# One level of Strassen's method for the two layers with 768 outputs, in a kernel of attention and two feed-forward layers

## The chip, the cores and the metric

The kernel runs on one core of a Trainium2 chip. The time is that of the device for one execution, in microseconds (us); of several runs the median is given.

## What is computed

```python
def reference(**kwargs):
    attn_out = _attn_ref(**attn_kwargs)          # causal attention, B=2, H=12, S=448, D=64
    x = np.ascontiguousarray(attn_out.transpose(0, 2, 1, 3)).reshape(B * S, H * D)
    x = _moe_ref(x=x, **moe_kwargs)
    return _moe2_ref(x=x, **moe2_kwargs)

def _moe_ref(x, w_in, w_out):                    # x 896 x 768, w_in 768 x 2048, w_out 2048 x 768
    h = x @ w_in
    g = h * np.clip(h + 3.0, 0.0, 6.0) / 6.0
    return (g @ w_out).astype(np.float32)

def _moe2_ref(x, w_gate, w_val, w_out, rms_g):   # w_gate, w_val 768 x 1536, w_out 1536 x 768
    rms = np.sqrt(np.mean(x * x, axis=-1, keepdims=True) + 1e-06)
    xn = x / rms * rms_g
    g = xn @ w_gate
    return (g * (1.0 / (1.0 + np.exp(-g))) * (xn @ w_val) @ w_out).astype(np.float32)
```

The weights arrive in float64, the rest in float32.

## The kernel before

The 896 tokens are two groups g of 448: the first and the second halves of both sequences. Activations lie transposed, tiles of 128 features x 448 tokens. A product in float32 accuracy is three matmuls on rounded halves (`mm3`, lines 179 to 188: hi x hi, hi x lo, lo x hi), each with a 128 x 128 weight tile and 448 columns.

The stages, in the order of `products` (line 472):

- attention, in 24 units of a pair of heads, one sequence and one group; the first matmuls of `ff1_in` are mixed in from the thirteenth unit on
- `ff1_in`: h = x w_in for group 0, then 1; 16 output tiles of 6 input tiles each; `ff1_relu`, `ff1_mul` form g, `ff1_high` and `ff1_low` split it into `ghi` and `glo`
- `ff1_out`: y = g w_out, group by group; 6 output tiles of 16 input tiles; `ff1_y` and `ff1_ylow` scale y by rms_g, split it, and POOL adds up its squares; `rms_sum`, `rms_root`, `rms_inv` form the inverse root
- `ff2_in`: gate and value (tile f), 12 x 2 x 2 output tiles of 6 input tiles; `ff2_gate`, `ff2_silu`, `ff2_val`, `ff2_high`
- `ff2_out`: 6 output tiles x 2 groups of 12 input tiles; `ff2_store`.

Weights come in pieces of 768 columns (six 128 x 128 tiles). `w_load` (line 107) loads float64; `w_split` turns it into float32 on ACT (Prelu for the high word, a byte operation for the low bits; for w_in that one is on POOL), `w_join` on DVE; `w_halves` (ACT) and `w_low` (DVE) make `whi` and `wlo`. The layers that go through their weights twice store the float32 pieces to DRAM (`w_keep`) and load them back for group 1.

The order is written out by hand. The program is built in steps; `at(delay, fn, ...)` records fn at a later step, and each step issues AFTER = 9 matmuls (BESIDE = 4.8 beside attention). A piece n is split one step after the first use of piece n - 3 (`w_tile`, line 169), halved a step later (two, where it has to be joined), its `wlo` made a step after that, and `w_low` asks for the next load. Every engine works its instructions off in this order, SP its DMA issues too; four buffers hold `whi` and `wlo`, three the raw pieces.

Of the kernel before, what the change touches and what calls it, by code (L numbers as in the profile page):

```python
# [9 lines left out]
F32 = mybir.dt.float32  # L10
# [11 lines left out]
NK = DM // 128  # L22
# [6 lines left out]
NSLOT = 82  # L29
# [3 lines left out]
BESIDE, AFTER = 4.8, 9  # L33
APART = 4
# [11 lines left out]
def fused_kernel(ctx: ExitStack, tc, qa, qb, ka, kb, v, w_in, w_out, w_gate, w_val, w_out2, rms_g, out):  # L46
# [53 lines left out]
    srcs, kept = [], {}  # L100
# [4 lines left out]
    srcs += [w_out2[n] for n in range(NF2)]  # L105
# [3 lines left out]
    state = {"load": 0, "split": 0}  # L109

    def w_load():
        n = state["load"]
        if n >= len(srcs):
            return
        state["load"] += 1
        if srcs[n] is None:
            c = wpool.tile([128, 768], F32, tag="c", name=f"c{n}", bufs=NC_BUF)
            nc.sync.dma_start(c, kept.pop(n))
            plain[n] = c
            return  # L120
        t = wpool.tile([128, 768, 2], U32, tag="raw", name=f"raw{n}", bufs=NRAW)
        nc.sync.dma_start(t.rearrange("p n t -> p (n t)"), srcs[n].bitcast(U32))
        raws[n] = t

    def w_split():
# [37 lines left out]
    def w_low(n, c):  # L163
        hi, lo = splits[n]
        nc.vector.tensor_sub(lo, c, f32(hi))  # L165
        if n >= NRAW:
            w_load()
# [11 lines left out]
    def mm3(ps, w, x, first, last):  # L179
# [3 lines left out]
        nc.tensor.matmul(ps, whi, xhi, start=first, stop=False)  # L183
        yield
        nc.tensor.matmul(ps, whi, xlo, start=False, stop=False)  # L185
        yield
        nc.tensor.matmul(ps, wlo, xhi, start=False, stop=last)  # L187
        yield


# [167 lines left out]
    def ff1_high(g, m, t):  # L358
        hi = slot([128, NT], f"ghi{g}_{m}", F32R)
        lo = slot([128, NT], f"glo{g}_{m}", F32R)  # L360
        nc.scalar.copy(hi, t)
        gs[g, m] = (hi, lo)
        at(1, ff1_low, hi, lo, t, nc.vector if g == 0 else nc.gpsimd)

    def ff1_low(hi, lo, t, engine=None):
        (engine or nc.gpsimd).tensor_sub(lo, t, f32(hi))  # L366

    def ff1_out(g, w0):

# [16 lines left out]

# [209 lines left out]
```

## Time and profile before

| | |
|---|---|
| median of 3 runs (lowest, highest) | 600.92 us (600.91, 601.79) |
| the profiled execution's own time | 601.82 us |
| its span, first to last instruction | 600.0 us |
| PE busy | 591.4 us, 99% |
| PE weight loads, DVE, ACT, POOL busy | 86%, 51%, 57%, 23% |
| mean granted TensorE clock | 0.997 of full speed |
| bytes moved by DMA | 92.98 MB, 155 GB/s over the span |

The profile is of one execution. Busy time of PE counts matmuls that overlap, so a row's mean duration is not the time between two of them. "Idle before" is the time an engine stood still just before the instructions of a row, with the engine, tile and line that ended most of it. The chain is followed back from the last instruction, at each step to what released it.

### The profile page before, as it was taken

The numbers are of one execution on the slowest core, as the hardware profiler recorded it, in microseconds if no ns is written. First come the engines' busy times: TensorE is split into PE (matmuls) and PEld (weight loads), VectorE is DVE, ScalarE is ACT, GpSimd is POOL, SyncE is SP. The second block draws the span as 40 slices with busy tenths as digits, with TensorE's granted clock in tenths as the row PEclk, the third lists the DMA queues.
The fourth block names the chain that finished last, engine by engine and source line by source line (L and its number), as shares of the span: only waits on it lengthen the run. The fifth ranks groups of instructions, "written<-read, shape, count | busy, mean of one in ns | idle before, by whom it ended". The sixth has DMA issues, their size and how long they took to land.

```text
span 600.0 us, 8836 instructions
## 1 busy us (share of the span) xinstructions
PE 591.4 (99%) x3192; PEld 518.8 (86%) x3192; DVE 307.2 (51%) x579; ACT 341.2 (57%) x652; POOL 137.7 (23%) x172
## 2 busy tenths in 40 slices
PE   8899999999999999999999999999999999999997
PEld 6557777778899999999999999999999999999996
DVE  4666767676444456563435565555544455333310
ACT  6998888787455688764335764445555544333300
POOL 4665454542033320010001011111111111000000
PEclk9999999999999999999999999999999999999999
DMA  8958776652233489863353433333333333344000
GB/s 222 277 192 253 226 247 217 215 182 85 74 108 116 182 306 330 319 226 124 101 185 140 154 128 117 112 117 107 106 106 105 106 105 106 121 139 148 32 32 31
DMA packets 32075, 92.98 MB, mean 155 GB/s; under 512 B 4640, under 2 KB 13792, under 8 KB 32032
## 3 DMA queue, kind: packets, MB, share of 16 engines
q1 hardware_dynamic: 31600, 92.08, 46.1%
q8 instruction: 25, 0.41, 0.3%
q10 hardware_dynamic: 432, 0.34, 0.2%
q14 instruction: 18, 0.15, 0.1%
HBM read 77.07 MB, written 15.34 MB: 154 GB/s over the span
## 4 chain that ended last, share of the span: by engine, by line
PE 94%; ACT 4%; POOL 1%; DVE 1%; issue 1%; POOLq 0%
PE f L183 10%; PE f L187 10%; PE f L185 10%; PE h L187 7%; PE y L183 7%; PE h L183 7%; PE h L185 7%; PE y L187 6%; PE y L185 6%; PE o L183 5%; PE o L187 5%; PE o L185 5%; PE s L241 3%; PE o L318 3%; PE t L292 3%; ACT sm L258 3%
## 5 line engine op out<-in xcount | busy, mean ns | idle before, releaser
L159 ACT CAST whi<-c 128x768 fp32r<-128x768 f32 x100 | 83.5, 835 | 89.5 <-DVE c L147 57.7
L165 DVE TENSOR_TENSOR wlo<-c,whi 128x768 fp32r<-128x768 f32 x100 | 99.7, 998 | 38.4 <-ACT whi L159 36.1
L183 PE MATMUL f<-yhi,whi 128*128 128x448 f32 x288 | 105.8, 367 | 0.0
L187 PE MATMUL f<-yhi,wlo 128*128 128x448 f32 x288 | 104.9, 364 | 0.0
L185 PE MATMUL f<-ylo,whi 128*128 128x448 f32 x288 | 104.0, 361 | 0.0
L147 DVE SCALAR_TENSOR_TENSOR c<-c,raw 128x768 uint32<-128x768 uint32 x68 | 66.9, 984 | 22.0 <-ACT raw L142 15.5
L187 PE MATMUL h<-xh,wlo 128*128 128x448 f32 x192 | 72.0, 375 | 0.0
L276 POOL TENSOR_SCALAR sm<-sm,st 112x112 f32<-112x112 f32 (+1 forms) x96 | 55.7, 598 | 69.1 <-ACT pt L302 28.3
L185 PE MATMUL h<-xl,whi 128*128 128x448 f32 x192 | 70.9, 369 | 0.0
L183 PE MATMUL y<-ghi,whi 128*128 128x448 f32 x192 | 70.5, 367 | 0.0
L183 PE MATMUL h<-xh,whi 128*128 128x448 f32 x192 | 70.4, 367 | 0.0
L187 PE MATMUL y<-ghi,wlo 128*128 128x448 f32 x192 | 70.0, 365 | 0.0
L185 PE MATMUL y<-glo,whi 128*128 128x448 f32 x192 | 69.3, 361 | 0.0
L366 POOL TENSOR_TENSOR slo<-u,shi 128x448 fp32r<-128x448 f32 x24 | 28.6, 1193 | 147.6 <-ACT shi L444 138.5
L138 ACT ACTIVATE c<-raw 128x768 f32<-128x768 f32 x68 | 61.4, 903 | 0.0
L187 PEld LDWEIGHTS f<-yhi,wlo 128*128 128x128 f32 x288 | 53.9, 187 | 5.4 <-issue 0.2
L185 PEld LDWEIGHTS f<-ylo,whi 128*128 128x128 f32 x288 | 54.1, 188 | 4.0
L183 PEld LDWEIGHTS f<-yhi,whi 128*128 128x128 f32 x288 | 54.1, 188 | 3.7 <-issue 0.2
L183 PE MATMUL o<-shi,whi 128*128 128x448 f32 x144 | 52.9, 367 | 0.0
L187 PE MATMUL o<-shi,wlo 128*128 128x448 f32 x144 | 52.3, 363 | 0.0
L258 ACT ACTIVATE sm<-sm,st 112x112 f32<-112x112 f32 (+3 forms) x96 | 49.7, 528 | 4.2 <-DVE st L251 4.2
L185 PE MATMUL o<-slo,whi 128*128 128x448 f32 x144 | 52.0, 361 | 0.0
(62 smaller groups left out, 866.9 us busy)
## 6 DMA issues: line engine op xcount, KB each, us to landing
raw<-in_w_out SPq DMA_DIRECT2D x28, 768.0 KB, 4.8
raw<-in_w_in SPq DMA_DIRECT2D x16, 768.0 KB, 5.5
kept<-c SPq DMA_DIRECT2D x32, 384.0 KB, 2.8
c<-kept SPq DMA_DIRECT2D x32, 384.0 KB, 3.1
raw<-in_w_gate SPq DMA_DIRECT2D x12, 768.0 KB, 4.3
raw<-in_w_val SPq DMA_DIRECT2D x12, 768.0 KB, 4.2
k<-in_kb SPq DMA_DIRECT2D x24, 112.0 KB, 4.6
v<-in_v SPq DMA_DIRECT2D x12, 224.0 KB, 3.6
```

Source lines behind the costliest of these rows:

```text
L138: nc.scalar.activation(c, f32(high), AF.Prelu, scale=2.0 ** -112, alpha=2.0 ** 32)
L147: nc.vector.scalar_tensor_tensor(bits, bits, 3, z, ALU.logical_shift_left, ALU.bitwise_or)
L159: nc.scalar.copy(hi, c)
L165: nc.vector.tensor_sub(lo, c, f32(hi))
L183: nc.tensor.matmul(ps, whi, xhi, start=first, stop=False)
L185: nc.tensor.matmul(ps, whi, xlo, start=False, stop=False)
L187: nc.tensor.matmul(ps, wlo, xhi, start=False, stop=last)
L241: nc.tensor.matmul(ps[:C, o:o + n], tq[64 * j:64 * j + 64, i * C:(i + 1) * C], tk[64 * j:64 * j + 64, 0:n], start=True, stop=True)
L258: nc.scalar.activation(dst, dst, AF.Exp, scale=-1.0, bias=st[u][:, 0, c:c + 1], accum_out=st[u][:, 1, c:c + 1])
L276: nc.gpsimd.tensor_scalar(t[:, o:o + n], t[:, o:o + n], c, 1.0, op0=ALU.mult, op1=ALU.mult)
L292: nc.tensor.transpose(banks[-1][:C, o:o + C], t[:, o0 + kc * C:o0 + (kc + 1) * C], ident[:C, :C])
L366: (engine or nc.gpsimd).tensor_sub(lo, t, f32(hi))
```

## The change

Both layers with 768 outputs are computed by one level of Strassen's method (in Winograd's form). The matrix of activations is cut by token group and by the parity of its input tiles, the weights by the parity of input tile and output tile. For a pair p of input tiles, A11 and A12 are the even and the odd tile of group 0, A21 and A22 those of group 1. The sums s1 = A21 + A22, s3 = A11 - A21, s2 = s1 - A11, s4 = A12 - s2 are formed on POOL (`sums_first`, `sums_second`, `sums_third`). Seven products replace eight: q = 1: A11 B11; 2: A12 B21; 5: s1 (B12 - B11); 6: s2 times B22 less the block of 5; 7: s3 times the block of 6 less B11; 3: s4 B22; 4: A22 times B21 less the block of 6. They stand outermost (ORDER1, ORDER2), each over 3 pairs n of output tiles and all input tiles of a parity; `combine` adds them up on DVE, or lets them accumulate in the same PSUM bank.

The float64 weights are turned to float32 once, cut by parity and kept in DRAM (`b_prepare`, `b_narrow`, `b_join`, `b_keep`): w_out beside attention and `ff1_in`, w_out2 beside `ff2_in`. A piece of a product is then one load, or two loads and a subtraction on POOL (tile pair); the blocks of products 5 and 6 are stored for later use. Pieces of `ff1_out` have 512 columns. The split of the activations moves from right behind their making to a product ahead (`a_split`, `a_low`; tiles `ahi`, `alo`).

```diff
-NSLOT = 82
+WIDE1, HALVES1 = 512, 2
+WIDE2 = 768
+ORDER1 = (1, 2, 5, 6, 7, 3, 4)
+ORDER2 = (1, 5, 6, 7, 3, 4, 2)
+BLOCKS = {1: (1,), 2: (2,), 3: (22,), 5: (12, 1), 6: (22, 5), 7: (6, 1), 4: (2, 6)}
+PREP1, APART1 = 108, 3.5
+NSLOT = 78
...
-    for a in (w_in, w_out):
-        srcs += [a[n] for n in range(NP1)] + NP1 * [None]
+    srcs += [w_in[n] for n in range(NP1)] + [("in", n) for n in range(NP1)]
+    srcs += [(1, p, n, h) for p in ORDER1 for n in range(NN) for h in range(HALVES1)]
...
+        return wpool.tile([128, 768, 2], U32, tag="raw", name=name, bufs=NRAW + 1)
...
+            for p in BLOCKS[q]:
+                found.append(kept[stage, p, k][:, h * wide:(h + 1) * wide])
...
+            t = f32(raw_tile(f"pair{n}").rearrange("p n t -> p (n t)"))
+            both = [t[:, :wide], t[:, 768:768 + wide]]
+        for t, src in zip(both, found):
+            nc.sync.dma_start(t, src)
+        plain[n] = both
...
-            at(1, w_halves, n, plain.pop(n))
+            c, *other = plain.pop(n)
+            if other:
+                nc.gpsimd.tensor_sub(c, c, other[0])
+                stage, q, k, h = srcs[n]
+                if q in (5, 6):
+                    at(1, b_keep, stage, q, k, h * c.shape[1], c)
+            at(1, w_halves, n, c)
...
+    def b_narrow(stage, column, first, raw, wide, beside):
+        narrowed(f32(raw[:, :wide, 1]), raw, beside)
+        at(1, b_join, stage, column, first, raw, wide)
...
+    def b_keep(stage, p, n, o, t):
...
+        nc.sync.dma_start(kept[stage, p, n][:, o:o + wide], t)
...
-        at(1, ff1_high, g, m, t)
+        left1[g, m] = t
+        if g == 1 and m % 2 == 1:
+            at(1, sums_first, left1, m // 2)
...
+    def a_split(left, q, p):
...
+        nc.scalar.copy(hi, src)
+        halves[which, q, p] = (hi, lo)
+        at(1, a_low, left, q, p, key, hi, lo, src)
+
+    def a_low(left, q, p, key, hi, lo, src):
+        nc.vector.tensor_sub(lo, src, f32(hi))
...
+    def strassen(which, order, kps, w0, pieces, after):
...
+        for i, q in enumerate(order):
+            if i + 1 < len(order):
+                for p in range(kps):
+                    at(LEAD[which] + p, a_split, left, order[i + 1], p)
+            for n in range(NN):
...
+                for p in range(kps):
+                    w = w_tile(w0 + (i * NN + n) * pieces + p // per, p % per)
+                    yield from mm3(ps, w, halves[which, q, p], first and p == 0, p == kps - 1, not first)
...
+                at(1, combine, which, q, n, ps, after)
...
+        elif q == 4:
+            t = held.pop(("f", n))
+            nc.vector.tensor_add(t, ps, t)
+            at(1, after, 1, 2 * n, t)
...
-                    for k in range(NK):
-                        yield from mm3(ps, w_tile(w0 + 2 * m + n, k), ys[g, k], k == 0, k == NK - 1)
+                    ks = (1, 3, 5, 0, 2, 4)
+                    for k in ks:
+                        yield from mm3(ps, w_tile(w0 + 2 * m + n, k), ys[g, k], k == ks[0], k == ks[-1])
...
-        yield from ff1_out(0, 2 * NP1)
-        yield from ff1_out(1, 3 * NP1)
-        yield from ff2_in(4 * NP1)
-        yield from ff2_out(4 * NP1 + 2 * NF2)
+        yield from strassen(1, ORDER1, NF1 // 2, OUT1, HALVES1, ff1_y)
+        for i in range(2 * NK):
+            at(6 + 6 * i, b_prepare, 2, w_out2, i // 2, i % 2, False)
+        yield from ff2_in(IN2)
+        yield from strassen(2, ORDER2, NF2 // 2, OUT2, 1, ff2_store)
...
+        for i in range(3 * NK):
+            column = (0, 2, 4, 1, 3, 5)[i // 3]
+            plan[int(PREP1 + APART1 * i)].append((0, b_prepare, 1, w_out, column, i % 3, column % 2 == 0))
```

How the instructions stand. First POOL in `ff1_out`, before: behind the low halves of g it only has the sums of squares (tile sq).

```order
L366 TENSOR_TENSOR glo1_14_2719<-t1_14_2686,ghi1_14_2718 128x448
L366 TENSOR_TENSOR glo1_15_2756<-t1_15_2724,ghi1_15_2755 128x448
L394 TENSOR_TENSOR sq0_0_2811<-sq0_0_2811,sq0_1_2895 128x448
L394 TENSOR_TENSOR sq0_0_2811<-sq0_0_2811,sq0_2_2990 128x448
L394 TENSOR_TENSOR sq0_0_2811<-sq0_0_2811,sq0_3_3074 128x448
```

And POOL there now, from the last sum of activations (line 498) on through the pieces 44 to 50, of the products 5 and 6:

```order
L498 TENSOR_TENSOR t0_15_2198<-t0_15_2198,t0_14_2141 128x448
L165 TENSOR_TENSOR pair44_3032<-pair44_3032 128x512
L165 TENSOR_TENSOR pair45_3056<-pair45_3056 128x512
L603 TENSOR_TENSOR sq0_0_3040<-sq0_0_3040,sq0_2_3108 128x448
L165 TENSOR_TENSOR pair46_3080<-pair46_3080 128x512
L165 TENSOR_TENSOR pair47_3127<-pair47_3127 128x512
L603 TENSOR_TENSOR sq0_0_3040<-sq0_0_3040,sq0_4_3180 128x448
L165 TENSOR_TENSOR pair48_3152<-pair48_3152 128x512
L165 TENSOR_TENSOR pair49_3175<-pair49_3175 128x512
L165 TENSOR_TENSOR pair50_3219<-pair50_3219 128x512
```

POOL now has a subtraction of two weight blocks for each piece of the products 5, 6, 7 and 4, and some sums of squares stand between them.

Second DVE at the handover from `ff1_out` to `ff2_in`, before (c66 and c67 are the second and third piece of `ff2_in`, ylo1_5 the last low half of y):

```order
L165 TENSOR_TENSOR wlo65_3650<-c65_3624,whi65_3649 128x768
L147 SCALAR_TENSOR_TENSOR c66_3652<-c66_3652,raw66_3590 128x768
L165 TENSOR_TENSOR wlo66_3679<-c66_3652,whi66_3678 128x768
L389 SCALAR_TENSOR_TENSOR ylo1_5_3700<-y1_5_3586,gvec_74,yhi1_5_3681 128x448
L147 SCALAR_TENSOR_TENSOR c67_3685<-c67_3685,raw67_3637 128x768
L428 TENSOR_TENSOR t0_0_3717<-f0_0_0_3669,sq0_0_2811 128x448
```

DVE there now; piece 74 is the first of `ff2_in`, v1_1 the bank of product 4 for the second pair of output tiles, e1_1 its result:

```order
L215 TENSOR_TENSOR wlo73_3909<-pair73_3848,whi73_3908 128x512
L190 SCALAR_TENSOR_TENSOR c74_3928<-c74_3928,raw74_3885 128x768
L576 TENSOR_TENSOR e1_1_2926<-v1_1_3878,e1_1_2926 128x448
L617 RECIPROCAL sq0_0_3040<-sq0_0_3040 128x448
L190 SCALAR_TENSOR_TENSOR c75_3944<-c75_3944,raw75_3902 128x768
L215 TENSOR_TENSOR wlo74_3958<-c74_3928,whi74_3957 128x768
L597 SCALAR_TENSOR_TENSOR ylo1_2_3980<-e1_1_2926,gvec_74,yhi1_2_3960 128x448
```

And ACT there now:

```order
L588 ACTIVATE yhi1_0_3904<-e1_0_2859,gvec_74 128x448
L590 ACTIVATE sq1_0_3906<-e1_0_2859 128x448
L209 CAST whi73_3908<-pair73_3848 128x512
L181 ACTIVATE c74_3928<-raw74_3885 128x768
L185 ACTIVATE raw74_3885<-raw74_3885 128x768
L613 ACT_TABLE_LOAD
L613 ACTIVATE sq0_0_3040<-n0_3920,eps_73 128x448
L181 ACTIVATE c75_3944<-raw75_3902 128x768
L185 ACTIVATE raw75_3902<-raw75_3902 128x768
L209 CAST whi74_3957<-c74_3928 128x768
```

The reciprocal of group 0, whose square root stands on ACT in front of `whi74`, has moved to between the join and the low half of `ff2_in`'s first piece; before, that of group 0 stood far ahead of this handover.

## Rows read from the trace of the kernel before

**Rows 1.** The page: busy time of the engines, and the chain that ended last.

```profile
PE 591.4 (99%) x3192; PEld 518.8 (86%) x3192; DVE 307.2 (51%) x579; ACT 341.2 (57%) x652; POOL 137.7 (23%) x172
...
PE 94%; ACT 4%; POOL 1%; DVE 1%; issue 1%; POOLq 0%
```

**Rows 2.** By stage: length, busy PE, PEld, DVE, ACT, POOL; clock, DMA share, GB/s.

```profile
47.00:155.00 108.00, 108.00 (x710) 83.31 (x708) 74.36 (x175) 86.10 (x203) 47.20 (x57) 1.00 0.61 196
155.00:216.00 61.00, 61.00 (x302) 56.56 (x303) 28.33 (x39) 34.72 (x55) 19.12 (x14) 1.00 0.43 143
216.00:333.00 117.00, 117.00 (x579) 108.15 (x578) 60.10 (x63) 66.80 (x92) 13.27 (x11) 1.00 0.61 213
333.00:509.00 176.00, 176.00 (x871) 162.84 (x870) 90.31 (x121) 91.87 (x127) 28.65 (x24) 1.00 0.33 112
509.00:597.00 88.00, 87.52 (x433) 80.80 (x431) 24.93 (x32) 20.93 (x28) 1.15 (x1) 1.00 0.24 83
```

**Rows 3.** Matmuls of tiles y and f (first, last start); rms in the chain.

```profile
L183 PE MATMUL y<-ghi,whi x192: 367/367/368, 216.3 to 332.9; 128*128 128x448 f32 x192
...
L183 PE MATMUL f<-yhi,whi x288: 367/367/368, 333.5 to 508.4; 128*128 128x448 f32 x144
...
281.77 0.75 PE n L400 x2
```

**Rows 4.** Groups by line and shape: busy, mean ns | idle before, releasers.

```profile
L165 DVE TENSOR_TENSOR wlo<-c,whi 128x768 fp32r<-128x768 f32 x100 | 99.7, 998 | 38.4 <-ACT whi L159 36.1
L159 ACT CAST whi<-c 128x768 fp32r<-128x768 f32 x100 | 83.5, 835 | 89.5 <-DVE c L147 57.7 <-PE y L185 19.3 <-PE o L185 11.2
...
L147 DVE SCALAR_TENSOR_TENSOR c<-c,raw 128x768 uint32<-128x768 uint32 x68 | 66.9, 984 | 22.0 <-ACT raw L142 15.5 <-POOL raw L140 3.5 <-ACT c L138 2.7
L138 ACT ACTIVATE c<-raw 128x768 f32<-128x768 f32 x68 | 61.4, 903 | 0.0
...
L142 ACT ACTIVATE raw<-raw 128x768 uint32<-128x768 uint8 x52 | 46.1, 887 | 0.0
...
L366 POOL TENSOR_TENSOR slo<-u,shi 128x448 fp32r<-128x448 f32 x24 | 28.6, 1193 | 147.6 <-ACT shi L444 138.5 <-DMA raw<-in_w_val 9.1
...
L366 DVE TENSOR_TENSOR glo<-t,ghi 128x448 fp32r<-128x448 f32 x16 | 9.9, 618 | 1.9 <-ACT ghi L361 1.7
...
L382 ACT ACTIVATE yhi<-y,gvec 128x448 fp32r<-128x448 f32 x12 | 7.5, 628 | 17.2 <-PE y L187 17.2
...
L384 ACT ACTIVATE sq<-y 128x448 f32<-128x448 f32 x12 | 6.4, 531 | 0.0
L408 DVE RECIPROCAL sq<-sq 128x448 f32<-128x448 f32 x2 | 5.9, 2953 | 6.2 <-ACT sq L404 6.2
...
L404 ACT ACT_TABLE_LOAD x2 | 2.6, 1283 | 0.0
...
L404 ACT ACTIVATE sq<-n,eps 128x448 f32<-128x448 f32 x2 | 1.3, 636 | 2.4 <-PE n L400 2.3
```

**Rows 5.** DMA: busiest stretch (columns as above); kept blocks to landing; a raw load.

```profile
230.00:250.00 20.00, 20.00 (x101) 18.54 (x100) 12.12 (x13) 14.56 (x21) 2.32 (x2) 1.00 0.94 340
...
DMA to landing us min/median/max: 2.3/3.0/6.0
...
raw<-in_w_gate SPq DMA_DIRECT2D x12, 768.0 KB, 4.3
```

**Rows 6.** POOL and DVE at once: all `glo` (ns), then instructions (start, length).

```profile
L366 POOL TENSOR_TENSOR glo<-t,ghi x16: 1157/1394/1418, 163.9 to 220.3; 128x448 fp32r<-128x448 f32 x16
...
181.54 0.96 DVE L165 TENSOR_TENSOR wlo<-c,whi 128x768 fp32r<-128x768 f32 x1
...
182.12 1.39 POOL L366 TENSOR_TENSOR glo<-t,ghi 128x448 fp32r<-128x448 f32 x1 [2.25 <-ACT ghi L361]
...
349.28 1.17 POOL L366 TENSOR_TENSOR slo<-u,shi 128x448 fp32r<-128x448 f32 x1 [13.19 <-ACT shi L444]
...
349.76 1.17 DVE L438 TENSOR_TENSOR u<-u,t 128x448 f32<-128x448 f32 x1
```

More of the change, by code (lines that the diff above doesn't have):

```diff
@@ L33 @@
 BESIDE, AFTER = 4.8, 9
+LEAD = {1: 2, 2: 1}
 APART = 4
@@ L177, in w_tile, with mm3 @@
         return tuple(t[:, j * 128:(j + 1) * 128] for t in splits[n])
-    def mm3(ps, w, x, first, last):
+    def mm3(ps, w, x, first, last, again=False):
         whi, wlo = w
         xhi, xlo = x
-        nc.tensor.matmul(ps, whi, xhi, start=first, stop=False)
+        nc.tensor.matmul(ps, whi, xhi, start=first, stop=False, skip_group_check=again)
         yield
-        nc.tensor.matmul(ps, whi, xlo, start=False, stop=False)
+        nc.tensor.matmul(ps, whi, xlo, start=False, stop=False, skip_group_check=again)
@@ L186, in mm3, with b_prepare, b_next @@
         yield
-        nc.tensor.matmul(ps, wlo, xhi, start=False, stop=last)
+        nc.tensor.matmul(ps, wlo, xhi, start=False, stop=last, skip_group_check=again)
         yield
+    def b_prepare(stage, src, column, part, beside):
+        queue.append((stage, src, column, part, beside))
+        b_next()
+    queue = []
+    def b_next():
+        if not queue:
+            return
+        free = state["raws"] <= NRAW if NP1 <= state["load"] < OUT1 + 6 else not state["preps"]
+        if not free:
+            at(1, b_next)
+            return
+        stage, src, column, part, beside = queue.pop(0)
+        tiles = src.shape[0] * 6 // NK
+        first = 6 * part
+        count = min(6, tiles - first)
+        state["preps"] += 1
+        raw = raw_tile(f"braw{stage}_{column}_{part}")
+        a = column * tiles + first
+        done = 0
+        while done < count:
+            piece, o = divmod(a + done, 6)
+            more = min(6 - o, count - done)
+            nc.sync.dma_start(
+                raw[:, done * 128:(done + more) * 128].rearrange("p n t -> p (n t)"),
+                src[piece][:, o * 128:(o + more) * 128].bitcast(U32))
+            done += more
+        at(3, b_narrow, stage, column, first, raw, count * 128, beside)
@@ L191, in fused_kernel @@
+    def b_keep(stage, p, n, o, t):
+        if (stage, p, n) not in kept:
+            kept[stage, p, n] = dram.tile([128, {1: NF1, 2: NF2}[stage] * 64], F32, name=f"kept{stage}_{p}_{n}")
+            parts[stage, p, n] = 0
+        wide = t.shape[1]
+        assert parts[stage, p, n] == o
+        nc.sync.dma_start(kept[stage, p, n][:, o:o + wide], t)
+        parts[stage, p, n] = o + wide
     units = [(g, b, p) for g in range(2) for p in range(NP) for b in range(B)]
@@ L426, in ff2_gate @@
     def ff2_gate(g, m, ps):
+        if g not in inverse:
+            at(1, ff2_gate, g, m, ps)
+            return
         t = slot([128, NT], f"t{g}_{m}")
```

223 lines of the change are left out of this document (160 added, 63 removed).

## The prediction

> **What bounds the kernel now.** I read the page's busy shares and the chain that ended last first [rows 1]: TensorE is busy for 99% of the span and carries 94% of the chain. Then a table by stage [rows 2], cut where the matmul tiles change name: attention with the first layer's first half (47 to 155 us), the rest of `ff1_in` (to 216), `ff1_out` (to 333), `ff2_in` (to 509), `ff2_out`. From 47 us on PE is busy in every microsecond, at the full clock; DVE and ACT are busy for half of `ff1_out` and less later, POOL for a tenth. So four of the five stages end when PE has issued its matmuls, and a matmul taken out there is worth its whole spacing. That spacing is not the 367 ns of a row, since matmuls overlap. Tile y starts at 216.3 us and f at 333.5 us, 576 matmuls later, with 0.75 us of rms matmuls between [rows 3]: (117.2 - 0.75) / 576 = 0.2022 us.
>
> **What the change takes away.** `ff1_out` is 2 groups x 6 x 16 x 3 = 576 matmuls and becomes 7 products x 3 x 8 x 3 = 504; `ff2_out` goes from 432 to 7 x 3 x 6 x 3 = 378. All keep 448 columns. 126 matmuls x 0.2022 = **25.5 us**, all of it on the path, if nothing new makes PE wait. (The Trainium skill, "TensorE: Matmul & The Clock Gate", Back-to-back issue gap, gives N/2.4 + 2.5 ns, here 189 ns, as an isolated gap; by it, an estimate, the saving would be 23.8 us. The trace's 0.2022 us is what this kernel pays, so it is used.)
>
> **What it adds, piece by piece.** The weights of `ff1_out` now come as 42 pieces of 512 columns, each used by 12 matmuls (2.43 us), those of `ff2_out` as 21 of 768, 18 matmuls (3.64 us). Before, one piece of 768 lasted 3.64 us.
>
> *Attention.* Six preparations of w_out fall into its end: for each a Prelu on ACT (0.90 us [rows 4]) and a byte operation on POOL. The `ghi0` casts leave ACT in the same stage, and POOL is busy for 47 of 108 us [rows 2]. Cost 0; if that cover fails, norms on POOL come late by one byte operation, about 1 us.
>
> *`ff1_in`, second half.* POOL gets three additions per pair of tiles (3 x 1.19 us [rows 4] = 3.6 us in 7.3 us) beside the rest of the preparations, one per 6.4 us. Free: nothing on PE reads these sums until the third product. Cost 0.
>
> *`ff1_out`, transfers.* In the products 5 and 6 a piece needs two loads and one store of 256 KB, 0.79 MB in 2.43 us = 323 GB/s for 29 us. The busiest stretch before moved 340 GB/s at a share of 0.94 [rows 5]. So the queue is just enough. A pair's load goes out when the pair three pieces ahead has been subtracted, 7.3 us minus about 1.6 us before it is wanted, and kept blocks landed in 3.0 us (2.3 to 6.0) [rows 5]. Cost 0; beyond a landing time of 5.7 us it delays each pair.
>
> *`ff1_out` and `ff2_out`, POOL beside DVE.* This is the cost I am least sure of. [Rows 6] show that POOL's subtraction takes 1.16 us alone, but 1.39 us when DVE's `wlo` (two inputs in SBUF) began 0.58 us before it, and that DVE's `u<-u,t` took 1.17 us instead of 0.62 when it began inside a POOL subtraction: the later one waits for nearly all of the overlap, some 0.15 us less. The Trainium skill, "SBUF — State Buffer", Who interferes with whom, says the same as a rule: a DVE instruction with two SBUF inputs and a GpSimd one that reads SBUF hold one port in turn. It speaks against this change, which puts 36 large POOL subtractions between just such DVE instructions. By rows [rows 4, 6]: a product of `ff1_out` with pairs has 6 subtractions of 512 columns (1.16 x 512/448 = 1.33 us), 6 `wlo` (0.69 us, between 0.62 and 1.00 by columns) and 8 `alo` (0.62 us): 8.0 + 4.1 + 5.0 = 17.1 us in turn, against 14.6 us of PE time; 0.15 us less at each of some 14 meetings leaves 15.0. Two square sums of 1.16 us join in product 5. Over the products 5, 6 and 7 that is 3 to 10 us too much, and the pairs start with a lead of some 5 us (`whi` may be written once the piece four ahead is done). In `ff2_out` a product is 3 x 1.99 + 3 x 1.00 + 6 x 0.62 = 12.7 us, or 11.3 us with the overlaps, against 10.9, but its first three pairs are ready early. Between 0 and 7 us in all; I take **0.5 us**, near the lower end, because every meeting in the rows is shorter than the sum by about the overlap I subtract.
>
> *From `ff1_out` to `ff2_in`.* Here the order of the queues costs something I can price. Product 4 ends with v_0, v_1, v_2. On ACT stand, in a row: `yhi` and square of v_0, `whi73`, Prelu and byte of raw74, the table load, the square root of group 0, Prelu and byte of raw75, `whi74`; on DVE the reciprocal, the join of c75, then `wlo74`, the third operand that f needs. From v_0's end [rows 4]: addition 0.62, `yhi` 0.63, square 0.53, `whi73` 0.57 (0.84 for 768 columns), Prelu 0.90, byte 0.89, table 1.28, root 0.64, reciprocal 2.95, join 0.98, `wlo` 1.00 = 11.0 us. PE needs it 48 matmuls plus 2 later: 50 x 0.2022 = 10.1 us. raw75 is asked for once `wlo71` has freed its buffer, a piece before that `yhi`, and such a load landed in 4.3 us before [rows 5], so it is not what ends last. PE waits about **1.0 us** (0 if ACT's starts overlap as PE's do, 3 if a landing is late). Queued behind: `wlo75`, not needed for another 7 us, and `ylo` of v_2, needed 34 matmuls into f and ready about as early.
>
> *End.* The last product still ends with a copy of two halves and two stores. 0.
>
> **Sum.** 25.5 - 0.5 - 1.0 = 24.0 us. The profiled execution took 601.82 us for a span of 600.0; it comes to 577.8, span 576.0. The median of the runs, 600.92, is 0.90 lower, so the forecast for the median is **576.9 us**.
>
> **Rivals.**
> 1. *The bare sum.* ACT and DVE run far enough ahead that nothing waits: 600.92 - 25.5 = 575.4 us. For it: [rows 2] show PE busy in every microsecond now, though the handover from y to f has the same kinds of steps. Against: the 11.0 us above. It lies at the end of the forecast's own range.
> 2. *POOL and DVE in turn become the bound of both Strassen stages.* If meetings cost their whole overlap, up to 10 - 5 = 5 us in `ff1_out` and 2 us in `ff2_out` are lost on top of the 1.0: 583.4 us at most, near 581. For it: 17.1 us of work in 14.6 us. Against: the 0.15 us less at every meeting in [rows 6]. (Taken strictly, the rule of "SBUF — State Buffer" in the Trainium skill, by which the later one fully blocks, gives this case; the trace agrees up to that 0.15 us.)
> 3. *Slower: the round trip through DRAM.* Products 6 and 7 read blocks that product 5 and 6 wrote; on SP the read waits for the write to land, and everything behind it on SP too. With a landing time L, a pair in `ff1_out` loses (L - 5.7) / 3 us, 24 of them; in `ff2_out` six reads stand one behind the other, each L + 1 us (the 1 for issuing) against 3.64, less two pieces of lead, 7.3 us. 8 (L - 5.7) + 6 (L - 2.6) - 7.3 reaches 25.5 at L = 6.7 us: from there the kernel is slower than before, at 8 us by 18 us (619 us). For it: the load is at the edge of what the queue did, and single transfers took 6.0 us. Against: a median of 3.0 us over all of them [rows 5].
> 4. *The change does not do what it says.* PE's rows fall by exactly 126, so only a slower matmul could hide it, and operands and widths are the same: 1 in 100.
>
> **How the numbers follow.** Forecast with rival 1 (waits of 0 to 3.5 us, 575.4 to 579): 0.72. Rival 2 (579 to 584): 0.16. A milder rival 3, landings of 5.8 to 6.7 us (584 to 601): 0.06. Rival 3 in full, slower: 0.04. Faster than the bare sum: 0.02. The range 575.0 to 583.0 leaves out a tenth above and little below. A difference of 0.2% (1.2 us) is about what a measurement of this kernel can tell from none. Faster by more 0.95, within 0.01, slower 0.04.
>
> **What would show it.** 504 + 378 = 882 matmuls of the tiles v, w, x, y and z; the spacing still 0.2022 us; `ff1_out` 102 us long and `ff2_out` 76.5 us. PE's only waits after 155 us: about 1 us for `wlo74` at the start of f, and some tenths for `whi` or `wlo` of pairs. Rival 2 would show POOL's subtractions of 512 columns well above 1.4 us, DVE's `alo` well above 0.62 and PE waiting from piece 50 on. Rival 3 would show SP's waits on a store of kept blocks, landings above 6 us and POOL idle for loads. A span above 579 or a changed spacing would make the forecast wrong.

## The result, and the profile after

The changed kernel takes **608.54 us** (median of 8 runs, 605.33 to 610.70); the kernel before, run beside it, 601.40 us (8 runs, 600.85 to 601.79). The ratio is 1.0115, 95% interval 1.0087 to 1.0142: **slower by 1.2%**, where 576.9 us was forecast, and outside the range. The profiled execution after took 607.03 us for a span of 605.2, so spans stand for times here as they did before. One execution of the last run below (791.55 us, mean granted clock 0.656) and one of the kernel before beside it (1485.67 us) stand far off all others and are left out of the ratios.

First the page, its busy times and its chain, to be held against [rows 1]:

```profile
PE 575.2 (95%) x3066; PEld 495.5 (82%) x3066; DVE 428.2 (71%) x733; ACT 359.7 (59%) x714; POOL 239.7 (40%) x233
...
PE 59%; DMA 13%; DVE 13%; ACT 6%; issue 4%; POOL 3%; SPq 1%; POOLq 0%; ACTq 0%; DVEq 0%
```

PE has lost the 126 matmuls (3192 to 3066) and 16 us of busy time, but it no longer carries the chain: 94% has become 59%, and DMA, DVE and ACT have come in. The stages of [rows 2], cut again where the matmul tiles change name (columns as there: length, busy time and count of PE, PEld, DVE, ACT, POOL, then granted clock, DMA share, GB/s), show where:

```profile
45.90:155.00 109.10, 109.10 (x715) 84.30 (x714) 68.88 (x168) 82.19 (x192) 50.36 (x61) 1.00 0.72 231
155.00:221.80 66.80, 61.87 (x300) 55.48 (x299) 45.97 (x61) 36.09 (x57) 30.26 (x24) 1.00 0.71 234
221.80:344.30 122.50, 110.29 (x508) 95.68 (x507) 109.15 (x125) 69.61 (x129) 66.92 (x46) 0.97 0.67 222
344.30:523.90 179.60, 177.25 (x867) 163.57 (x866) 113.03 (x155) 98.93 (x134) 35.96 (x24) 0.99 0.56 196
523.90:602.00 78.10, 76.90 (x379) 70.62 (x378) 61.85 (x74) 32.22 (x55) 28.00 (x14) 1.00 0.48 164
```

Before, PE was busy in every microsecond from 47 to 509 us. Now it has gaps in the second half of `ff1_in` (61.87 us busy of 66.80) and above all in `ff1_out`: 122.5 us for 504 matmuls that need 504 x 0.2022 = 101.9. DVE, which was busy for half of that stage, is busy for 109.15 of its 122.50 us, and the granted clock, 1.00 in every stage before, is 0.97. From the first matmul of h to that of x (y before), then to f, then to w (o before) and to the end of the span:

| stage, us | before | bare sum of the forecast | after | lost |
|---|---|---|---|---|
| `ff1_in` (beside attention at first) | 169.3 | 169.3 | 175.9 | 6.6 |
| `ff1_out` with the handover | 117.2 | 102.6 | 122.5 | 19.9 |
| `ff2_in` | 175.5 | 175.5 | 179.6 | 4.1 |
| `ff2_out` and the end | 91.0 | 80.1 | 81.3 | 1.2 |

(The bare sum takes 72 and 54 matmuls of 0.2022 us from the stages before.) 31.8 us were lost where 25.5 were saved; h also began 1.1 us earlier, which makes up the 5.2 us between the two spans.

Two things stand out in the trace. The groups by line and shape (busy, mean ns | idle before, releaser) answer to [rows 4] and [rows 6]:

```profile
L215 DVE TENSOR_TENSOR wlo<-c,whi 128x768 fp32r<-128x768 f32 x65 | 67.4, 1037 | 9.5 <-ACT whi L209 9.5
L516 DVE TENSOR_TENSOR alo<-t,ahi 128x448 fp32r<-128x448 f32 x48 | 48.7, 1020 | 0.0
...
L516 DVE TENSOR_TENSOR alo<-s,ahi 128x448 fp32r<-128x448 f32 x20 | 20.5, 1042 | 0.0
...
L165 POOL TENSOR_TENSOR pair<-pair 128x512 f32<-128x512 f32 x24 | 36.2, 1513 | 25.3 <-DMA pair<-kept 25.1
```

`alo` has the shape of `glo` on DVE, which took 618 ns before; it takes 1020 to 1042. POOL's pair subtraction of 512 columns takes 1513 ns, where the forecast scaled it to 1.33 us. Single instances show who waits for whom (timeline of the profile after; start, length, engine, instruction):

```profile
288.19 0.62 DVE L516 TENSOR_TENSOR alo<-t,ahi 128x448 fp32r<-128x448 f32 x1
288.76 1.29 POOL L165 TENSOR_TENSOR pair<-pair 128x512 f32<-128x512 f32 x1 [1.87 <-DMA pair<-kept]
289.26 1.28 DVE L516 TENSOR_TENSOR alo<-t,ahi 128x448 fp32r<-128x448 f32 x1
...
335.15 1.75 POOL L165 TENSOR_TENSOR pair<-pair 128x512 f32<-128x512 f32 x1
335.67 0.61 DVE L576 TENSOR_TENSOR e<-v,e 128x448 f32<-128x448 f32 x1
```

The `alo` that began before POOL's subtraction keeps its 0.62 us; the one that began inside it takes 1.28 us, 0.66 more for an overlap of 0.79. So it is all through this profile: an `alo` that the timeline lists singly takes 0.61 or 0.62 us if it meets nothing on POOL or began first, and 1.18 to 1.90 us if it began inside a two-input instruction of POOL. The addition `e<-v,e`, which has only one input in SBUF (v is a PSUM bank), lies wholly inside a subtraction and still takes 0.61 us.

And the waits (engine and line, for whom: us in total, times, longest) show a new family of waits, for the weight blocks on their way:

```profile
POOL pair L165 <- DMA pair<-kept: 47.6, 23, 5.9
ACT braw L181 <- DMA braw<-in_w_out: 46.4, 16, 6.5
...
POOL braw L183 <- DMA braw<-in_w_out: 30.7, 8, 9.1
...
DVE b L285 <- POOL braw L183: 18.5, 5, 6.4
```

One instance of the `braw` waits can be followed through all engines (timeline of 150 to 163.4 us; start, length, engine, instruction, idle before it and its releaser; each engine's rows apart):

```profile
152.05 0.32 SPq L153 DMA_DIRECT2D c<-keptin  x1
152.80 0.81 SPq L269 DMA_DIRECT2D braw<-in_w_out  x2
...
154.75 0.43 SPq L269 DMA_DIRECT2D braw<-in_w_out  x1
...
159.16 0.91 ACT L181 ACTIVATE braw<-braw 128x768 f32<-128x768 f32 x1 [6.10 <-DMA braw<-in_w_out]
159.96 0.82 ACT L209 CAST whi<-c 128x768 fp32r<-128x768 f32 x1
160.68 0.34 ACT L437 CAST xh<-o 128x224 fp32r<-128x224 f32 x1
...
159.22 0.87 POOL L183 TENSOR_SCALAR braw<-braw 128x768 uint32<-128x768 uint8 x1 [9.15 <-DMA braw<-in_w_out]
...
150.11 1.04 DVE L285 SCALAR_TENSOR_TENSOR b<-braw 128x384 uint32<-128x384 uint32 x2 [3.40 <-POOL braw L183]
151.06 0.96 DVE L215 TENSOR_TENSOR wlo<-c,whi 128x768 fp32r<-128x768 f32 x1
...
160.15 1.03 DVE L285 SCALAR_TENSOR_TENSOR b<-braw 128x384 uint32<-128x384 uint32 x2 [6.45 <-POOL braw L183]
...
161.08 0.47 PE L235 MATMUL h<-xh,whi 128*128 128x448 f32 x1 [0.91 <-ACT xh L437]
162.70 0.47 PE L237 MATMUL h<-xl,whi 128*128 128x448 f32 x1 [1.16 <-DVE xl L443]
```

The load goes out in two pieces from 152.80 us on (the one at 154.75 is the next block's). ACT comes to it at 153.06 us, 0.3 us after SP began to issue it, although three steps lie between the two in the written order: SP had itself stood for 6.3 us, up to its load at 152.05, for DVE's `wlo` (151.06), which stood behind a `b` of the block before (150.11), late in the same way. One late block thus delays the load of the next. ACT is 6.1 us, POOL 9.15 us too early and both stand; nothing that is behind in their order starts meanwhile. PE needs nothing of `braw`. It needs `xh`, which stands two instructions behind the waiting one on ACT, and `xl` behind `b` on DVE, and so it waits twice.

From here three theories went to the chip. **A**: POOL's two-input work and DVE's two-input work shut each other out, and DVE, full in `ff1_out`, feeds PE late. **B**: blocks come late; B1, the preparations' loads have not landed when ACT and POOL reach them (the row above), or B2, the round trip through DRAM (store, wait, load), the forecast's rival 3. **C**: what is left follows from single stalls, such as the one at f, and from the lower granted clock after them.

### The profile page after: what moved, and what is told of

Read it like the earlier page. It is cut to its first block, busy times and chain, and to the rows that moved or that the text cites. A ratio compares the mean times of both kernels' runs of the same rounds, so it can differ in the third digit from the quotient of the medians.

```text
span 605.2 us, 9154 instructions
## 1 busy us (share of the span) xinstructions
PE 575.2 (95%) x3066; PEld 495.5 (82%) x3066; DVE 428.2 (71%) x733; ACT 359.7 (59%) x714; POOL 239.7 (40%) x233
## 4 chain that ended last, share of the span: by engine, by line
PE 59%; DMA 13%; DVE 13%; ACT 6%; issue 4%; POOL 3%; SPq 1%; POOLq 0%; ACTq 0%; DVEq 0%
PE f L239 10%; PE f L237 10%; PE f L235 10%; DMA braw<-in_w_out 7%; DVE wlo L215 5%; DVE alo L516 4%; PE s L350 4%; DMA pair<-kept 3%; PE t L401 3%; PE o L427 3%; PE h L239 3%; DMA kept<-pair 3%; PE h L237 3%; PE h L235 3%; ACT sm L367 2%
## 5 line engine op out<-in xcount | busy, mean ns | idle before, releaser
L209 ACT CAST whi<-c 128x768 fp32r<-128x768 f32 (+1 forms) x83 | 65.3, 787 | 52.0 <-DVE c L190 40.8
L215 DVE TENSOR_TENSOR wlo<-c,whi 128x768 fp32r<-128x768 f32 (+1 forms) x83 | 84.0, 1013 | 9.5 <-ACT whi L209 9.5
L165 POOL TENSOR_TENSOR pair<-pair 128x512 f32<-128x512 f32 (+1 forms) x36 | 61.9, 1724 | 54.1 <-DMA pair<-kept 47.6
L285 DVE SCALAR_TENSOR_TENSOR b<-braw 128x384 uint32<-128x384 uint32 (+1 forms) x60 | 41.9, 739 | 30.3 <-POOL braw L183 18.5
L209 ACT CAST whi<-pair 128x512 fp32r<-128x512 f32 (+1 forms) x36 | 24.8, 692 | 55.3 <-POOL pair L165 45.5
L181 ACT ACTIVATE braw<-braw 128x768 f32<-128x768 f32 (+1 forms) x30 | 25.8, 861 | 47.8 <-DMA braw<-in_w_out 46.4
L215 DVE TENSOR_TENSOR wlo<-pair,whi 128x512 fp32r<-128x512 f32 (+1 forms) x36 | 39.9, 1108 | 13.2 <-ACT whi L209 13.2
L516 DVE TENSOR_TENSOR alo<-t,ahi 128x448 fp32r<-128x448 f32 x48 | 48.7, 1020 | 0.0
L239 PEld LDWEIGHTS h<-xh,wlo 128*128 128x128 f32 x192 | 36.1, 188 | 12.2 <-issue 6.7
L190 DVE SCALAR_TENSOR_TENSOR c<-c,raw 128x768 uint32<-128x768 uint32 x40 | 39.1, 978 | 7.9 <-ACT c L181 3.2
```

The source lines that it names most:

```text
L165: nc.gpsimd.tensor_sub(c, c, other[0])
L239: nc.tensor.matmul(ps, wlo, xhi, start=False, stop=last, skip_group_check=again)
L285: nc.vector.scalar_tensor_tensor(t.rearrange("p (k c) -> p k c", c=128).bitcast(U32), pairs[:, :, odd, :, 1], 3, pairs[:, :, odd, :, 0], A ...
L516: nc.vector.tensor_sub(lo, src, f32(hi))
```

## The experiments

### First set: each suspect alone

**Without the subtraction** (the pair's first block is used alone):

```diff
             if other:
-                nc.gpsimd.tensor_sub(c, c, other[0])
                 stage, q, k, h = srcs[n]
```

> Leaves out the 36 subtractions of two weight blocks on POOL (a pair's first block is used as it came); loads, stores and all else stay. The changed kernel loses 6 us of PE time in ff1_in, 20.6 in ff1_out, 4.1 in ff2_in and 1.3 in ff2_out. Theory A (POOL's subtractions and DVE's two-input instructions shut each other out; alo took 1.02 us in the mean for 0.62): wlo of 512 columns back near 0.69 us and alo near 0.65 once the sums of activations are done; ff1_out loses under 12 us, time 608.5 -> 595 to 600. Theory B (transfers come late, and the queues stand behind them): ff1_out keeps over 16 us of its loss, time within 5 us of 608.5.

Measured: 597.0 us, ratio to before 0.9926 (0.9892 to 0.9960), 11.5 us less than the changed kernel. `ff1_out` falls to 110.7 us, `alo<-t` to 799 ns. In its profiled run `ff1_in` was even longer (181.9 us) with 52.9 us of ACT's waits for `braw`, so a second loss is left that this edit does not touch.

**The narrowing later** (six steps of the order behind its load, not three, and all preparations six steps earlier so that the last ones are still in time):

```diff
-PREP1, APART1 = 108, 3.5
+PREP1, APART1 = 102, 3.5
...
-        at(3, b_narrow, stage, column, first, raw, count * 128, beside)
+        at(6, b_narrow, stage, column, first, raw, count * 128, beside)
```

> The first two operations on a prepared block of w_out or w_out2 stand 6 steps behind its load instead of 3, and the preparations of w_out begin 6 steps earlier so that the blocks are there in time. Theory B1 (ACT and POOL reach these operations before the load has landed, 5.0 us in the median, stand still, and DVE's wlo with them): PE's loss of 6 us in ff1_in falls under 2, that of the first two products of ff1_out from about 9 to under 5; time 608.5 -> 598 to 602. Theory A (POOL against DVE alone): within 3 us of 608.5.

Measured: 593.1 us, ratio 0.9861 (0.9841 to 0.9880): 15.4 us less, more than expected. `ff1_in` takes 169.3 us again, as before the change. The first row is that stage, the second `ff1_out`:

```profile
155.00:216.30 61.30, 61.30 (x304) 56.83 (x304) 50.56 (x62) 37.59 (x58) 32.19 (x24) 1.00 0.74 249
...
216.30:330.80 114.50, 105.67 (x508) 93.89 (x507) 108.63 (x120) 66.82 (x125) 63.85 (x43) 1.00 0.67 219
```

PE has no gap left in `ff1_in`, and of the waits for the loads of `braw` 12.1 us on POOL and 2.4 us on ACT remain. `ff1_out` is still 114.5 us, and there DVE is now busy for 95% of the time.

**Strassen in the second layer alone** (`ff1_out` as in the kernel before):

```diff
-    srcs += [w_in[n] for n in range(NP1)] + [("in", n) for n in range(NP1)]
-    srcs += [(1, p, n, h) for p in ORDER1 for n in range(NN) for h in range(HALVES1)]
+    for a, name in ((w_in, "in"), (w_out, "out")):
+        srcs += [a[n] for n in range(NP1)] + [(name, n) for n in range(NP1)]
...
-        yield from strassen(1, ORDER1, NF1 // 2, OUT1, HALVES1, ff1_y)
+        yield from ff1_out(0, OUT1)
+        yield from ff1_out(1, OUT1 + NP1)
```

> Strassen's method for the second layer with 768 outputs alone; the first one is computed as before the change. 54 matmuls fewer than before the change, 10.9 us. Theory A and theory B alike put the loss into ff1_in and ff1_out, where pieces last 2.43 us and the preparations stand beside two passes; what is left here is the 1.3 us of ff2_out and up to 1 us for the preparations of w_out2 beside ff2_in: 601.4 - 10.9 + 1.3 to 2.3 = 591.8 to 592.8. If the second stage only looked good because the first had delayed it, its loss grows and the time is above 595.

Measured: 591.97 us, ratio 0.9841 (0.9827 to 0.9856). 54 matmuls x 0.2022 = 10.9 us were to be had and 9.8 came (against 601.76 us of the kernel before on that chip): the method pays in `ff2_out` almost in full, with the same preparations (beside `ff2_in`, which stays at 175.5 us), pairs and transfers. The loss is the first layer's.

**No block read back soon after it was stored** (each pair is taken from blocks of the preparation, so none reads what a subtraction has just written):

```diff
-BLOCKS = {1: (1,), 2: (2,), 3: (22,), 5: (12, 1), 6: (22, 5), 7: (6, 1), 4: (2, 6)}
+BLOCKS = {1: (1,), 2: (2,), 3: (22,), 5: (12, 1), 6: (22, 12), 7: (22, 1), 4: (2, 22)}
```

> The products 6, 7 and 4 read, as their second or first block, blocks that have been in DRAM for long instead of those that product 5 and 6 stored; the stores themselves, the number and the size of all loads and all subtractions stay (the product is another one). Theory B2 (the store's way to DRAM and back holds SP, and with it the loads behind): SP's 30 us of waits on stores of pairs go, landing to subtraction gets shorter, ff1_out gains 3 to 8 us, time 608.5 -> 600 to 605. Theory A: the subtractions come as often as before, within 2 us of 608.5.

Measured: 607.58 us, ratio 1.0089 (1.0064 to 1.0114): no gain beyond 1 us. The edit takes away less than was expected of it: SP's waits for stores of pairs fall from 30.4 us to 18.6, not to nothing. What is left is bounded by the first run of the next set, where SP stands for such stores even longer (36.4 us) and `ff1_out` is only 2.1 us above the bare sum of 102.6. So B2 is no main cause here, although the chain of the changed kernel runs through stores and loads of such blocks for a while.

### Second set: is A separate from B1, and what is A?

All four start from the kernel with the narrowing later (593.1 us).

**Both edits together:** also without the subtraction.

> Narrowing later, as in the run before (593.1 us), and POOL's subtraction of the pairs left out (the pair's first block is used alone, so the result is not the layer's). It asks whether the two gains (11.5 and 15.4 us) are of two causes. Theory A (POOL's two-input subtractions hold up DVE's two-input ones, which are the full engine of ff1_out): ff1_out 114.5 us falls to 104 to 107 us, alo below 0.80 us, the whole 583 to 586 us. Rival (both edits cured the same loss, the late preparations): 591 to 593.5 us, ff1_out above 112 us.

Measured: 580.51 us, ratio 0.9643 (0.9629 to 0.9658), a little below the range expected. Another 12.6 us: two separate losses. `ff1_out` is 104.7 us, 9.8 less than with the narrowing later alone; `ff2_in`, 176.96 us in place of 179.63, gives 2.7 more: PE's wait at its start is shorter (1.07 us for 2.33) and the granted clock behind it stays at 1.00. `alo<-t` is at 801 ns, with the sums of activations still beside it.

**One input in place of two:**

```diff
-                nc.gpsimd.tensor_sub(c, c, other[0])
+                nc.gpsimd.tensor_scalar(c, c, 1.0, 0.0, op0=ALU.mult, op1=ALU.add)
```

> As the run with the narrowing later, but POOL's operation on a pair is c*1+0, of one input, in place of the subtraction of two: POOL still waits for both blocks' place in the order, still stands between load, whi and store, and works on the same 128x512 (the result is not the layer's). It tells the port from the chain. Theory A: what hurts DVE is the second operand, so the time is near that without the subtraction, 583 to 587 us, and alo is below 0.80 us. Rival (the step on POOL in the chain load, POOL, whi, store costs the time, whatever it does): 590 to 593.5 us with alo as low, DVE idle for POOL.

Measured: 585.16 us, ratio 0.9733 (0.9717 to 0.9749). POOL's instruction is still there, with its waits and its followers, and 7.9 us are gone. `alo` stays above the 0.80 us that was expected. The groups by line:

```profile
L516 DVE TENSOR_TENSOR alo<-t,ahi 128x448 fp32r<-128x448 f32 x48 | 39.8, 836 | 0.3 <-ACT ahi L511 0.3
...
L165 POOL TENSOR_SCALAR pair<-pair 128x512 f32<-128x512 f32 x24 | 19.6, 818 | 28.4 <-DVE alo L516 11.3 <-DMA pair<-kept 7.2 <-DVE wlo L215 4.0
```

The instruction of one input takes 818 ns where the subtraction took 1522 in the kernel it starts from. In the profiled execution, the fastest of the four (582.34 us), `ff1_out` is 104.7 us, as short as without any instruction on POOL, though POOL still stands between load and `whi`. The two profiles differ at f: 2.35 us of waiting here, for 1.07 there.

**The root later** (table load, square root and reciprocal of group 0 come five steps later):

```diff
-            at(2, rms_sum, g)
+            at(2 + 5 * (g == 0), rms_sum, g)
```

> Narrowing later, and the rms sum of group 0 five steps later, so that table load, root and reciprocal come behind wlo74 and wlo75 on ACT and DVE. Theory C (PE's wait of 2.3 us at f costs that wait and then some 1.6 us more at a granted clock of 0.88): both go, 593.1 falls by 3.5 to 4.1 us to 589 to 589.6 us, and no matmul of f is at the lower clock. Rival (the reciprocal then holds up the next piece instead): 592 to 594 us.

Measured: 589.11 us, ratio 0.9797 (0.9782 to 0.9811), 4.0 us less, as theory C has it. PE's wait at f is gone and the clock stays full; `ff2_in` takes 176.2 us in place of 179.6:

```profile
329.70:345.00 15.30, 15.30 (x74) 13.54 (x73) 10.46 (x12) 12.54 (x16) 3.00 (x2) 1.00 0.56 214
```

**One input everywhere** (the sums of activations too):

```diff
-        nc.gpsimd.tensor_add(t, left[1, 2 * p], left[1, 2 * p + 1])
+        nc.gpsimd.tensor_scalar(t, left[1, 2 * p], 1.0, 0.0, op0=ALU.mult, op1=ALU.add)
...
```

> As the run with the one-input operation for pairs, and POOL's sums of activations are one-input operations too (s = a*1+0 and so on; the result is not the layer's). Every instruction, wait and transfer is still there in its order; only POOL's second SBUF operand is gone. Theory A: nothing holds DVE up, alo 0.62 to 0.66 us, ff1_out 102 to 103 us, the whole 579 to 581.5 us (the bare sum 575.4 and about 4 us at the start of f). Rival (late blocks or DVE's count of instructions alone): above 588 us.

Measured: 582.09 us, ratio 0.9673 (0.9659 to 0.9688), `ff1_out` 104.4 us; a little above what A expected.

```profile
L516 DVE TENSOR_TENSOR alo<-t,ahi 128x448 fp32r<-128x448 f32 x48 | 34.2, 720 | 1.6 <-ACT ahi L511 1.6
L215 DVE TENSOR_TENSOR wlo<-pair,whi 128x512 fp32r<-128x512 f32 x24 | 19.3, 805 | 12.2 <-ACT whi L209 12.0
```

Here my wording of A was off. I expected `alo` to fall to its undisturbed 0.62 to 0.66 us; `alo<-t` stays at 720 ns. POOL's instructions of one input still disturb DVE; they only do so for about half as long. So the second operand on POOL is not what matters by itself; what fits all runs is the time for which POOL's instruction is under way when one of DVE's with two SBUF inputs comes up.

### Third set: a test that A must pass with work moved, not removed

If POOL's subtraction shuts DVE out for longer than DVE would need for it, then giving *more* work to the full engine must help. The first two kernels start from the one with the root later (589.1 us).

**The pairs on DVE:**

```diff
-                nc.gpsimd.tensor_sub(c, c, other[0])
+                nc.vector.tensor_sub(c, c, other[0])
```

> The run with the root later (589.1 us), and the subtraction of the pairs on DVE in place of POOL: nothing is left out. Theory A (a POOL subtraction of 512 columns shuts DVE's two-input instructions out for most of its 1.5 us, where DVE does it itself in some 0.7 us, as its wlo of the same shape): although DVE is the full engine and gets 36 instructions more, ff1_out falls from 113.9 to 104 to 107 us and the whole to 579.5 to 583 us. Rival (DVE is full by its own work, POOL's beside it costs little): 24 x 0.7 = 17 us more on DVE in ff1_out, 595 to 606 us.

Measured: 586.96 us, ratio 0.9763 (0.9745 to 0.9782). The sign is theory A's, since DVE got 36 instructions more and the time fell; the size is not: 2.1 us, not 6 to 9.6. `ff1_out` came to 109.3 us, and a new wait in `ff2_out` took back 2.9 us (84.2 in place of 81.3): DVE now stands itself for a pair's load (2.86 us idle up to 538.13 us, released by the DMA), with an `alo` behind it that PE waits for. That is theory B again, a block that has not landed when an engine comes to it, now on DVE.

**The sums on DVE as well** (`nc.gpsimd` becomes `nc.vector` in `sums_first`, `sums_second` and `sums_third`).

> As the run before with the pairs on DVE, and the sums of the activations too (32 of 448 columns in ff1, 24 in ff2, 0.62 us each in place of 1.3 to 1.7 on POOL). POOL keeps byte operations and square sums. Theory A: between 577 and 583 us, within 3 us of the run before, since each sum takes DVE 0.62 us where it now shuts it out for about 1.2. Rival: DVE has 35 us more of its own, 590 us and above.

Measured: **582.05 us**, ratio 0.9686 (0.9667 to 0.9705), the fastest of the kernels that keep all the work (the last run below is not to be told from it), 3.1% below the kernel before. `ff1_out` is 107.4 us. Not all of the 4.9 us to the run before comes from the sums: of the two profiles `ff1_out` gives 1.9 us, and `ff2_out` (84.2 to 80.0) gives 4.2, because the wait for a pair's load did not come up there; POOL is busy for 6.3 us of that stage in the one, at its start, and not at all in the other. Groups by line:

```profile
L516 DVE TENSOR_TENSOR alo<-t,ahi 128x448 fp32r<-128x448 f32 x48 | 30.4, 634 | 0.0
...
L215 DVE TENSOR_TENSOR wlo<-pair,whi 128x512 fp32r<-128x512 f32 x24 | 17.3, 723 | 0.0
L165 DVE TENSOR_TENSOR pair<-pair 128x512 f32<-128x512 f32 x24 | 16.8, 700 | 7.8 <-DMA pair<-kept 7.5 <-issue 0.2
```

and the stage:

```profile
216.20:323.60 107.40, 103.80 (x506) 93.93 (x506) 96.57 (x155) 65.71 (x122) 12.51 (x8) 1.00 0.71 228
```

With POOL nearly silent (12.51 us) DVE's instructions have nearly their own length again: `alo` 634 ns, the subtraction 700 ns where POOL needed 1522 in the run with the narrowing later. With 35 more instructions in the stage than in the run with the narrowing later (155 for 120), DVE is busy for *less* time, 96.57 us in place of 108.63.

**Earlier preparations alone** (the changed kernel with PREP1 102, the narrowing still three steps behind the load).

> The change with one number altered: the preparations of w_out begin at step 102 in place of 108; their narrowing stays three steps behind the load. It divides the gain of the run that altered both (15.4 us). If what counts is that the narrowing comes before its load has landed, so that ACT and POOL stand in order: 603 to 608 us, POOL's and ACT's waits for braw still above 50 us together. Rival (it is the place of the preparations, which end in the first product): 593 to 598 us.

Measured: 610.38 us, ratio 1.0148 (1.0131 to 1.0165): nothing gained. Of the two numbers altered together above, the earlier start alone does nothing, so the distance between load and narrowing is what is needed; whether it is enough without the earlier start was not run. ACT and POOL stand as long as ever:

```profile
ACT braw L181 <- DMA braw<-in_w_out: 53.3, 19, 6.5
...
POOL braw L183 <- DMA braw<-in_w_out: 23.6, 7, 6.8
```

**Splits one step earlier**, on top of the best version (`LEAD = {1: 1, 2: 1}`).

> The run with pairs and sums on DVE (582.05 us) still waits twice for alo at the start of a product of ff1_out (0.69 and 0.92 us, at 281 and 312 us). Here the splits of a product's activations in ff1_out begin one step of the order earlier. If these waits are only the place of alo in DVE's order, both go: 579.5 to 581 us. If DVE is simply full there (busy 31.9 of 33.1 us from 274.5 us to 291 us and from 307 us to 323.6 us), the wait turns up elsewhere: 581.5 to 583 us.

Measured: 581.62 to 587.56 us in five executions, ratio 0.9688 (0.9663 to 0.9713) beside 0.9686 of the version it starts from: no difference that can be told. (The busy share quoted there is mis-added: 14.97 and 15.90 make 30.87 us of 33.1.) The profiled execution is the slowest of the five (587.56 us, `ff1_out` 109.5 us). The two waits for `alo` are gone from it; PE waits for `wlo` of pairs instead, 0.39, 0.76 and 1.68 us between 262 and 279 us. DVE stands 9.0 us for pairs' loads in `ff1_out`.

## Why the prediction was wrong, step by step

**Right:** 126 matmuls fewer, each worth 0.2022 us where nothing makes PE wait: from its first matmul of w to the end of its span the version with sums on DVE takes 80.0 us, the bare sum 80.1. The changed kernel's 81.3 there is near it too. Rival 3 was rightly given little: the run that read no fresh blocks gained 1 us at most, although landings did go up, from a median of 3.0 us [rows 5] to 4.1 us for kept blocks (1.9 to 8.2).

**The step "`ff1_in`, second half. Free: nothing on PE reads these sums until the third product. Cost 0"** (and "Attention. Cost 0") failed, and was the largest error: 15.4 us. I asked only whether the engines had *time* for the preparations, and they had. I did not ask what stands behind each of them in order when its operand is late. The narrowing was put three steps behind its load; the loads of w_out landed after 3.9 to 7.7 us (median 5.6), and already the load of [rows 5] took 4.3 us; with its issue held up on SP besides, ACT stood 46.4 us and POOL 30.7 for it, and PE waited for casts and splits behind. Shown by the narrowing later (15.4 us less, `ff1_in` back at 169.3) and by the earlier start alone (nothing). By stage the profiles give 6.6 us of it in `ff1_in` and 8.0 in `ff1_out`, 6.1 of these in the first two products (36.5 us, then 30.4), into which the late preparations ran, until 251.7 us.

**The term "`ff1_out` and `ff2_out`, POOL beside DVE: 0.5 us"** had the mechanism and missed the size: 12.6 us between the run with the narrowing later and the same without the subtraction. Of these, 9.8 us stand in `ff1_out`. The 0.15 us less at each meeting held (0.13 in the rows above), but it was no reason for a small sum, and four things were left out. I counted the products 5, 6 and 7, but product 4 has pairs too. I named only `wlo` and `alo` on DVE, which also has additions of 0.62 us and `ylo` to do in these products. A subtraction took 1.51 us, not 1.33. And I let a lead of 5 us pay for the rest. By the text's own figures in turn, 17.1 - 14.6 = 2.5 us for each of four products, 10 us, would have been near, but by luck: in the run with the narrowing later product 5 takes 17.5 us, 3.0 too long, and 6 and 7 together 31.5, 2.4 too long. The sums of activations were costed against PE alone, but they shut DVE out as the subtractions do: moving them to DVE brought `ff1_out` from 109.3 to 107.4 us. The Trainium skill, "SBUF — State Buffer", Who interferes with whom, states an exclusive lock between a DVE instruction of two SBUF inputs and a GpSimd instruction that reads SBUF. The trace agrees here, also for GpSimd instructions of one input (`alo` 720 ns beside them, 634 ns without), up to the 0.13 us by which the later instruction waits less than the overlap. I had that rule as rival 2 and gave it 0.16 and 583.4 us at most.

**The term "From `ff1_out` to `ff2_in`: about 1.0 us"** was right in its place and its chain, and too small. After, the chain from the addition to the end of `wlo74` took 335.67 to 347.15 us, 11.5 us for the forecast's 11.0. Its last part, DVE and then PE, and POOL's square sum (timeline, as above):

```profile
340.49 0.62 DVE L576 TENSOR_TENSOR e<-v,e 128x448 f32<-128x448 f32 x1
341.56 2.95 DVE L617 RECIPROCAL sq<-sq 128x448 f32<-128x448 f32 x1 [0.45 <-ACT sq L613]
344.43 0.90 DVE L190 SCALAR_TENSOR_TENSOR c<-c,raw 128x768 uint32<-128x768 uint32 x1
345.25 1.90 DVE L215 TENSOR_TENSOR wlo<-c,whi 128x768 fp32r<-128x768 f32 x1
...
344.99 1.33 POOL L603 TENSOR_TENSOR sq<-sq,sq 128x448 f32<-128x448 f32 x1 [5.93 <-ACT sq L590]
...
347.19 0.47 PE L239 MATMUL f<-yhi,wlo 128*128 128x448 f32 x1 [2.35 <-DVE wlo L215]
```

`wlo74` takes 1.90 us, not 1.00, since POOL's square sum began 0.26 us before it; the addition at the chain's start came late behind a stretched `wlo` of a pair. PE waits 2.35 us. Then something follows that I had not priced: the granted clock of 344.3 to 360 us is 0.89, 0.11 x 15.7 = 1.7 us more. The run with the root later got both back (4.0 us).

**The sum.** The three gains, 15.4 + 12.6 + 4.0 = 32.0 us, are about the 31.6 us by which the forecast failed. That they agree so closely is luck: the 12.6 us hold 2.7 us of `ff2_in` that the run with the root later counts again, so single terms are good to some 3 us. To the bare sum of 575.4 us, 33.1 us were lost, and 15.4 + 9.9 + 4.0 = 29.3 us of them are accounted for, each counted once.

What stays open: the 5 us that the best version still lacks to the forecast, of which its profile shows five waits of PE's in `ff1_out`, 3.6 us together, for DVE's `wlo` and `alo`; pairs' loads, for which DVE stands 7.5 us, are a likely cause that no run took away. And of the 9.8 us in `ff1_out`, how much is the shutting out and how much the length of POOL's step in the chain from load to `whi`: the one-input run gets all of them back with that step still in the chain, but it also shortens it, from 1522 to 818 ns. The single instances show that the shutting out is there; no run holds the length of the step fixed.

## What to carry to other kernels

Work that is moved onto an engine with time to spare is free only if its operands are there when the engine comes to it: for each added instruction look at the landing time of its load and at what stands behind it in order. Where the instructions of two engines wait for each other, as DVE's and POOL's with SBUF inputs do here, add up their times in turn, with all that either has to do; then the slower of the two should not do what the faster could do in half the time, even if the faster is the full one. Where an engine is busy for 95% of a stage, as DVE was in `ff1_out` (108.63 of 114.5 us), there is little room left for such waits before the engine that it feeds has to wait too.

## What the runs showed of the hardware

The lower clock after short waits. In the profile of the changed kernel, stretches right behind PE's waits (columns as above; the clock is the third number from the end):

```profile
242.30:250.00 7.70, 7.65 (x30) 6.81 (x31) 7.70 (x8) 5.17 (x10) 5.41 (x4) 0.78 0.52 179
324.00:330.00 6.00, 5.91 (x21) 5.35 (x22) 6.00 (x9) 3.10 (x6) 3.35 (x3) 0.72 0.24 87
347.20:354.00 6.80, 6.80 (x26) 6.19 (x27) 6.49 (x9) 5.23 (x7) 1.44 (x1) 0.75 0.75 233
```

Before them PE had waited 2.76, 2.24 and 2.35 us. A mean between 1.00 and one half says that part of each stretch ran at the lower of the two levels, 1.2 GHz; 26 matmuls took 6.80 us where 0.2022 us each would make 5.3. It is not a matter of the wait's length alone: in the run with the root later 1.99 us up to 310.30 were followed by 0.78, but in the run with earlier preparations 2.25 us up to 328.50 by 1.00, and 1.68 us up to 278.51 in the last run by 1.00. So a wait of some 2 us can cost more than itself (1.7 us behind the 2.35 us at f), and the kernel before, whose PE does not wait for any operand from 47 us on [rows 2], shows nothing of it there.
